# Memory attention and an erf-softplus feed-forward layer: the summed keys and values turned by VectorE's block transposes, phi's maxima spread through a row in device memory

## The chip, the core and the metric

The kernel runs on one core of a Trainium2 chip. The metric is the device time of one execution in microseconds; before the change it is 703.14 us, the median of 3 runs (702.33 to 703.39). One execution was also recorded by the hardware profiler; every time below that is not the median comes from that execution.

## What is computed

```python
def _attn_ref(q, k, v, phi):                 # batch 8, heads 8, seq 576, head_dim 64, 32 memories
    a = phi - np.max(phi, axis=2, keepdims=True)
    a = np.exp(a)
    a = a / (np.sum(a, axis=2, keepdims=True) + 1e-09)
    k_m = np.einsum('bhsm,bhsd->bhmd', a, k)
    v_m = np.einsum('bhsm,bhsd->bhmd', a, v)
    scores = scale * np.matmul(q, k_m.transpose(0, 1, 3, 2))     # scale = 1/8
    scores = scores - np.max(scores, axis=-1, keepdims=True)
    attn = np.exp(scores)
    attn = attn / (np.sum(attn, axis=-1, keepdims=True) + 1e-09)
    return np.matmul(attn, v_m)
def _moe_ref(x, w_in, w_out):                # 4608 tokens, 512 -> 2048 -> 512
    h = x @ w_in
    sp = np.maximum(h, 0.0) + np.log1p(np.exp(-np.abs(h)))
    return (h * erf(sp)) @ w_out
```

For each batch and head, 32 weights per position (softmax of phi over the sequence) condense keys and values to 32 "memories"; the queries attend to these; the result goes through a two-layer network.

## The kernel before

The 8 batches are worked on one after the other in 16 steps each (128 steps in all): step k makes 128 of the 2048 hidden columns for the 576 positions of a batch. For a step TensorE makes `psh` (first layer, `ffn1`, line 794), ScalarE or VectorE copies it to `h` (lines 811, 812), ScalarE takes softplus and erf in groups of four steps (lines 829, 834), VectorE multiplies and splits the product into a rounded part and a remainder, `g_hi` and `g_lo` (lines 860 to 863), and some steps later TensorE adds the product with `w_out` into `pso`, one accumulator for each 128 positions (`ffn2`, line 871). The last 64 positions of two batches share `psr`. At a batch's end ScalarE copies each `pso` to a tile `ot` (line 931), and SyncE stores it; `ot` lies in the two buffers of the pool `phiT`.

Keys, values and phi of batch b are prepared while earlier batches run through the steps:

- VectorE takes phi's maxima `pmx` (line 502), for 128 rows (four heads of 32 memories) in each of two halves `g`. ScalarE spreads each along a row of 128 (`bias`, line 507), TensorE transposes the two halves (line 527), so that in PSUM the maxima of a head and memory stand in a column of every partition, and VectorE adds them to the phi that has the positions in the partitions (line 533); ScalarE takes exp (line 536).
- TensorE sums keys and values with these weights (`psa<-kv,phi`, line 621). ScalarE divides by the sum and writes each of the sums twice side by side (`kvk`, line 647). TensorE transposes four 128x128 blocks of it (line 653), and ScalarE copies the result out of PSUM into `km` (times the scale 1/8) and `vm` (line 678), two buffers each, one for each parity of b.
- From `km` TensorE makes the scores (`psa<-q,km`, line 691), VectorE turns them (line 739) and makes the softmax; from `vm` and `w_in` TensorE makes `vw` (line 691 too), which is split for the first layer.

The order on every engine is made ahead by a planner (`Plan.order`): each operation has a cost and a rank, and of those that are ready the one with the lowest rank goes next; a table of numbers moves single operations in rank. Each engine then executes its instructions strictly in this order, and each DMA is issued from SyncE's queue in its order.

Of the kernel before, what the change touches and what calls it, by code (L numbers as in the profile page):

```python
# [32 lines left out]
ROW = 116  # L33
# [215 lines left out]
def tile_memory_attention_then_erf_softplus_ffn(  # L249
# [36 lines left out]
    LAG = 6  # L286
    FR1, FR2 = 4, 6
    IN_PSUM = 1
    TAIL = 3
# [3 lines left out]
        for n, b, kw in (  # L293
# [7 lines left out]
            ("g", 3, {}),  # L301
            ("raw", RAW, {}),
            ("ps", 4, {"space": PSUM}),
            ("po", 1, {"space": PSUM}),
# [3 lines left out]
    room = {"wo": NPR, "vw_hi": 2, "vw_lo": 2, "at": 8, "h": HB, "e": EB}  # L308
    room.update({"g_hi": 3, "g_lo": 3, "raw": RAW, "ps": 4, "sc": 2, "dk": 1, "bias": 1, "phiT": 2})
    room.update({f"pso{d}": 1 for d in range(NT)})  # L310
# [43 lines left out]
    rest = const.tile([P, NK, 2, P], F32R, name="rest")  # L354
    km = [const.tile([P, NP_, M], F32, name=f"km{i}") for i in range(2)]
    vm = [const.tile([P, NP_, M], F32, name=f"vm{i}") for i in range(2)]
    w_in_sb = [const.tile([P, NP_, 512], F32, name=f"w_in{p}") for p in range(4)]
# [140 lines left out]
    def phi_sums(rank, b):  # L498

        for g in range(NG):  # L500
            t, mx = ("phiT", b, g), tile_(f"pmx{g}", "pmx", b, g)
            op(DVE, on_dve(S), rank, [t], [mx], lambda t=t, mx=mx: nc.vector.reduce_max(  # L502
                out=get(mx), in_=get(t), axis=AX.X, negate=True))
        if b:
            bias = tile_("bias", "bias", b, shape=[P, NG, P], pool="att")
            for g in range(NG):
                op(ACT, 320, rank, [("pmx", b, g)], [(bias, g)], lambda g=g: nc.scalar.activation(
                    get(bias)[:, g], ident, AF.Identity, scale=0.0, bias=get(("pmx", b, g))))
# [10 lines left out]

    def phi_numbers(rank, b):  # L520

        a, bias = ("phi", b), ("bias", b)
# [16 lines left out]
    def memories(rank, rank_2, b, parts):  # L539
# [3 lines left out]
        if b:  # L543
            together(rank, phi_numbers(rank, b))
        else:
# [7 lines left out]
        for turn_n, part in enumerate(parts):  # L553
            first, second = sums_and_turn(rank_2 + turn_n * 0.01, b, part)
            together(rank_2 + turn_n * 0.01, first)
            together(rank_2 + turn_n * 0.01, second)

    bundles = []

    def together(rank, *pieces, kind="small"):  # L560
# [35 lines left out]
    def sums_and_turn(rank, b, part, rank_2=None, into=None):  # L596
# [32 lines left out]
        kvs = [("kv", b, x, g) for g, x in part]  # L629

        def first():
            if into is None:
                tile_("ps", *ps, shape=[P, 4, P], pool="ps")
            tile_("dk", *t, shape=[P, 4, 2, D], pool="att")
            yield
            yield n_g * NC * 110 * n_x, [a] + kvs, [ps] if into is None else [(k, "sums") for k in banks], [t], sums
            for n, g in enumerate(gs):
                rs = ("prs", b, g)

                def keep(f, n=n):  # L640
                    return lambda: f(
                        get(t)[:, n * n_x : (n + 1) * n_x],
                        sums_of(n).rearrange("p (x d) -> p x d", d=D).unsqueeze(2)
                        .to_broadcast([P, n_x, 2, D]))

                op(ACT, on_act(2 * n_x * D, True), rank, [ps if into is None else (banks[n], "sums"), rs], [(t, n)],
                   keep(lambda y, x, rs=rs: nc.scalar.activation(y, x, AF.Identity, scale=get(rs))),
# [33 lines left out]

        return first(), second()

# [40 lines left out]
    def attention(rank, rank_2, u, more=0):  # L724
# [13 lines left out]
        for g in range(NG):  # L738
# [7 lines left out]
        op(ACT, on_act(S), rank_2, [s], [s],  # L746
           lambda: nc.scalar.activation(get(s), get(s), AF.Exp), kind="exp")
        op(DVE, on_dve(S), rank_2, [s], [sm], lambda: nc.vector.reduce_sum(
# [245 lines left out]

    def alone(rank, x):
        together(rank, x, kind=None)

# [28 lines left out]
    for b in range(1, B):  # L1026
        o = NK * b
        if b == 1:
            PARTS += [
                (o + 1, [(phi_numbers, 2), (vw, 1, 4)]),  # L1030
                (o + 5, [(sums[2],), (vw, 1, 8)]),
                (o + 5, [(turn[2],)]),
                (o + 9, [(attention, 4), (vw, 1, 12)]),
# [13 lines left out]
    for n, fs in PARTS:  # L1047
        when(int(n), bundle, at(n), fs)
    for b in range(1, B, 2):
        for k in range(0, NK, 2):  # L1050
# [25 lines left out]
    for n, d in {  # L1076
# [10 lines left out]
    }.items():  # L1087
        plan.ops[n].rank += d
    for n, e in {
        324: ACT, 382: ACT, 476: ACT, 516: ACT,  # L1090
    }.items():
        plan.ops[n].ways = {e: plan.ops[n].ways[e]}
# [64 lines left out]
```

## Time and profile before

| | |
|---|---|
| median of 3 runs | 703.14 us (702.33 to 703.39) |
| the profiled execution | 702.5 us |
| its span | 700.7 us |
| TensorE busy (matmul) | 694.5 us, 99% of the span |
| ScalarE busy | 490.7 us, 70% |
| VectorE busy | 451.5 us, 64% |
| DMA | 66.71 MB, mean 95 GB/s |

The span goes from the first to the last instruction of the program; the execution's own time has 1.8 us more around it. "Busy" is the union of an engine's recorded instructions. Matmuls overlap each other in the records: one starts long before the one ahead of it has ended, so what a matmul costs is seen from the distance between starts, not from its recorded length.

### The profile page before, as it was taken

The page shows a single profiled execution, that of the slowest core. Times are in us where ns is not written, and L with a number is a line of the kernel's source. Part 1 is how long each engine was busy: PE and PEld are TensorE (multiplying, and loading weights), DVE is VectorE, ACT ScalarE, POOL GpSimd, SP SyncE. Part 2 cuts the span into 40 slices and gives each one's busy share as a digit, 9 for nine tenths or more (in the row PEclk, how much of TensorE's full clock was granted, in tenths as well). Part 3 has the DMA queues.
Part 4 walks back from the last instruction along what each step waited for, and adds up shares of the span by engine and source line. Part 5 has one row for each costly group of instructions (what it writes and reads, how often), then busy time and mean ns, then how long its engine had stood idle before and what let it go on. Part 6 is the DMA issues. An engine that isn't in the chain of part 4 may idle for free.

```text
span 700.7 us, 12333 instructions
## 1 busy us (share of the span) xinstructions
PE 694.5 (99%) x4866; PEld 562.8 (80%) x4866; DVE 451.5 (64%) x779; ACT 490.7 (70%) x797; POOL 105.9 (15%) x262
## 2 busy tenths in 40 slices
PE   8999999999999999999999999999999999999997
PEld 4566778788887888878888788878888788888886
DVE  4999999687744567685554747665565258546530
ACT  4899998967766678788655777586576557566821
POOL 0024111111101111121111110211111012111110
PEclk9999999999999999999999999999999999999999
DMA  9999131615103041113310323010010100000002
GB/s 362 415 417 415 53 125 52 236 36 198 59 1 102 7 189 46 54 64 108 116 35 0 110 98 136 24 61 1 2 50 19 61 16 1 1 37 24 1 1 75
DMA packets 19993, 66.71 MB, mean 95 GB/s; under 512 B 2272, under 2 KB 2528, under 8 KB 19936
## 3 DMA queue, kind: packets, MB, share of 16 engines
q1 hardware_dynamic: 19504, 64.85, 25.0%
q10 hardware_dynamic: 432, 1.08, 0.4%
q8 instruction: 38, 0.62, 0.3%
q14 instruction: 19, 0.16, 0.1%
HBM read 56.49 MB, written 9.44 MB: 94 GB/s over the span
## 4 chain that ended last, share of the span: by engine, by line
PE 92%; DVE 4%; DMA 2%; ACT 1%; issue 0%
PE pso L871 50%; PE psh L794 28%; PE psr L871 6%; PE psa L691 5%; PE psa L621 2%; DMA q<-qT 2%; DVE w L453 1%; DMA phiT<-phiT 1%; PE psa L653 0%; DVE w L477 0%; DVE g L849 0%; DVE h L811 0%; DVE w_in L477 0%; DVE phi L533 0%; DVE pmx L502 0%
## 5 line engine op out<-in xcount | busy, mean ns | idle before, releaser
L871 PE MATMUL pso<-wo,g_hi 128*128 128x512 f32 x976 | 305.9, 395 | 0.1
L871 PEld LDWEIGHTS pso<-wo,g_hi 128*128 128x128 f32 x976 | 174.8, 188 | 44.2 <-issue 12.6
L871 PE MATMUL pso<-wo,g_lo 128*128 128x512 f32 x488 | 191.6, 393 | 0.0
L812 ACT ACTIVATE h<-psh 128x288 f32<-128x288 f32 x176 | 71.5, 410 | 116.0 <-PE psh L794 115.2
L867 POOL CAST rest<-g_hi 128x64 fp32r<-128x64 f32 x122 | 51.5, 424 | 435.8 <-DVE g_hi L862 420.4
L860 DVE TENSOR_TENSOR e<-e,h 128x576 f32<-128x576 f32 x122 | 90.6, 754 | 34.0 <-ACT e L834 33.6
L794 PE MATMUL psh<-at_hi,vw_hi 128*128 128x288 f32 x496 | 108.7, 300 | 0.0
L871 PEld LDWEIGHTS pso<-wo,g_lo 128*128 128x128 f32 x488 | 91.6, 188 | 21.0
L794 PE MATMUL psh<-at_lo,vw_hi 128*128 128x288 f32 x496 | 106.3, 296 | 0.0
L794 PE MATMUL psh<-at_hi,vw_lo 128*128 128x288 f32 x496 | 105.8, 295 | 0.0
L862 DVE CAST g_hi<-e 128x576 fp32r<-128x576 f32 x122 | 54.8, 454 | 76.5 <-PE pso L871 67.5
L794 PEld LDWEIGHTS psh<-at_hi,vw_hi 128*128 128x128 f32 x496 | 86.1, 188 | 17.2 <-issue 3.0
L863 DVE TENSOR_TENSOR g_lo<-e,g_hi 128x576 fp32r<-128x576 f32 x122 | 93.6, 771 | 6.3
L829 ACT ACTIVATE e<-h 128x576 f32<-128x576 f32 x127 | 86.3, 685 | 14.4 <-DVE g_lo L863 8.3
L834 ACT ACTIVATE e<-e 128x576 f32<-128x576 f32 x128 | 81.1, 678 | 0.4
L794 PEld LDWEIGHTS psh<-at_hi,vw_lo 128*128 128x128 f32 x496 | 79.9, 189 | 0.0
L794 PEld LDWEIGHTS psh<-at_lo,vw_hi 128*128 128x128 f32 x496 | 79.2, 188 | 0.0
L811 DVE COPY h<-psh 128x288 f32<-128x288 f32 x78 | 34.3, 449 | 38.7 <-PE psh L794 38.5
L867 POOL CAST rest<-g_lo 128x64 fp32r<-128x64 f32 x122 | 44.4, 365 | 92.1 <-DVE g_lo L863 90.2
L369 DVE TENSOR_TENSOR vw_lo<-psa,vw_hi 128x512 fp32r<-128x512 f32 (+1 forms) x68 | 41.1, 638 | 15.1 <-ACT vw_hi L367 15.1
L871 PE MATMUL psr<-wo,rest 128*128 128x512 f32 x192 | 46.1, 390 | 0.0
L367 ACT ACTIVATE vw_hi<-psa 128x512 fp32r<-128x512 f32 (+1 forms) x68 | 34.3, 562 | 14.5 <-PE psa L691 14.5
(83 smaller groups left out, 646.3 us busy)
## 6 DMA issues: line engine op xcount, KB each, us to landing
kv<-kv SPq DMA_DIRECT2D x31, 640.0 KB, 8.5
w<-w_in SPq DMA_DIRECT2D x8, 1023.8 KB, 14.8
w<-w_out SPq DMA_DIRECT2D x8, 1023.8 KB, 14.6
q<-qT SPq DMA_DIRECT2D x28, 288.0 KB, 3.1
out<-ot SPq DMA_DIRECT2D x31, 256.0 KB, 2.2
phi<-phi SPq DMA_DIRECT2D x7, 640.0 KB, 4.5
phiT<-phiT SPq DMA_DIRECT2D x15, 288.0 KB, 3.0
q<-qT SPq DMA_DIRECT2D x2, 576.0 KB, 10.3
```

Source lines behind the costliest of these rows:

```text
L367: lambda: nc.scalar.activation(get_hi(), get_src(), AF.Identity))
L369: lambda: nc.vector.tensor_tensor(out=get_lo(), in0=get_src(), in1=get_hi().bitcast(F32), op=ALU.subtract))
L691: nc.tensor.matmul(out=get(ps[par])[p * M : (p + 1) * M, :n], lhsT=w[rows, p, :], rhs=x_of(rows, p), start=True, stop=True,)
L794: nc.tensor.matmul(out=get(ps)[:, :U], lhsT=x[:, g, k % 4 * P : (k % 4 + 1) * P], rhs=y[:, g, :], start=(n + g == 0), stop=(n == len(parts ...
L812: other={ACT: (on_act(U, True), lambda: nc.scalar.activation(keep(), get(ps), AF.Identity))})
L829: last[:] = [op(ACT, on_act(S), rank, [("h", i)], [e], lambda: nc.scalar.activation(get(e), get(("h", i)), AF.Softplus), kind="softplus", ...
L834: last[:] = [op(ACT, on_act(S), rank, [e], [e], lambda: nc.scalar.activation(get(e), get(e), AF.Erf), kind="erf", edge=edge, after=last)]
L860: op(DVE, on_dve(S), rank, [e, h], [e], lambda: nc.vector.tensor_tensor(out=get(e), in0=get(e), in1=get(h), op=ALU.mult))
L862: op(DVE, on_dve(S, 1), rank, [e], [hi], lambda: nc.vector.tensor_copy(out=get(hi), in_=get(e)))
L863: op(DVE, on_dve(S), rank, [e, hi], [lo], lambda: nc.vector.tensor_tensor(out=get(lo), in0=get(e), in1=get(hi).bitcast(F32), op=ALU.subtract))
L867: lambda x=x, y=y: nc.gpsimd.tensor_copy(out=rest[:, k, x, cols], in_=get(y)[:, NT * P :]))
L871: nc.tensor.matmul(out=o, lhsT=y, rhs=z, start=(start and n == 0), stop=(stop and n == len(parts) - 1))
```

## The change

For batches 2 to 7 (`TURNED = 2`) the four TensorE transposes of `kvk` and the four ScalarE copies out of PSUM are left out. ScalarE writes the sums once into `kvk`, not twice, and VectorE turns it by eight block transposes (32 partitions, 4 blocks of 32 each) straight into `kvm`, a tile that now holds km and vm side by side. The scale 1/8 moves into the exp of the scores. For batches 3 to 7 (`SPREAD = 3`) the maxima go through device memory: SyncE writes the two columns `pmx` into a `row` of 256 numbers, then loads it into all 128 partitions as `bias`; VectorE adds this from SBUF. ScalarE's two spreads and TensorE's two transposes for it are left out. The table of ranks and the list of engines are replaced.

```diff
+    TURNED, SPREAD = 2, 3
+            ("row", 2, {"space": bass.MemoryType.DRAM}),
-    km = [const.tile([P, NP_, M], F32, name=f"km{i}") for i in range(2)]
-    vm = [const.tile([P, NP_, M], F32, name=f"vm{i}") for i in range(2)]
+    kvm = [const.tile([P, 2, NP_, M], F32, name=f"kvm{i}") for i in range(2)]
+    km, vm = ([t[:, x] for t in kvm] for x in range(2))
...
-        if b:
+        if b >= SPREAD:
+            bias = tile_("bias", "bias", b, shape=[P, NG * P], pool="att")
+            row = tile_("row", "row", b, shape=[NG, P], pool="row")
+            for g in range(NG):
+                op(SP, 60, rank, [("pmx", b, g)], [(row, g)], lambda g=g: nc.sync.dma_start(
+                    out=get(row)[g].unsqueeze(1), in_=get(("pmx", b, g))), nbytes=P * 4)
+            op(SP, 60, rank, [row], [bias], lambda: nc.sync.dma_start(
+                out=get(bias), in_=get(row).rearrange("g p -> (g p)").unsqueeze(0)
+                .to_broadcast([P, NG * P])), nbytes=P * P * 8)
+        elif b:
...
+        if b < SPREAD:
+            return phi_numbers_turned(rank, b)
+        a, bias = ("phi", b), ("bias", b)
+        op(DVE, on_dve(NC * H * M), rank, [a, bias], [a], lambda: nc.vector.tensor_tensor(
+            out=get(a)[:ROW], in0=get(a)[:ROW],
+            in1=get(bias)[:ROW].unsqueeze(1).to_broadcast([ROW, NC, H * M]), op=ALU.add))
+        op(ACT, on_act(NC * H * M), rank, [a], [a], lambda: nc.scalar.activation(
+            get(a)[:ROW], get(a)[:ROW], AF.Exp), kind="exp")
...
+        def turned():
+
+            for j in range(4):
+                for d in range(2):
+                    to = slice((j % 2 * 2 + d) * 32, (j % 2 * 2 + d + 1) * 32)
+
+                    def emit(j=j, d=d, to=to):
+                        nc.vector.transpose(
+                            out=kvm[b % 2][to, :, j // 2 :: 2].rearrange("p x g m -> p g x m"),
+                            in_=get(t)[M * j : M * (j + 1), :, 0, d * 32 : (d + 1) * 32]
+                            .rearrange("p (g x) d -> p g x d", x=2))
+
+                    op(DVE, on_dve(4 * M), rank_2, [(t, n) for n in range(2)],
+                       [((name, b % 2), (j // 2, j % 2, d)) for name in ("km", "vm")], emit)
+
...
-        return first(), second()
+        return first(), turned if b >= TURNED else second()
...
-           lambda: nc.scalar.activation(get(s), get(s), AF.Exp), kind="exp")
+           lambda: nc.scalar.activation(get(s), get(s), AF.Exp, scale=SCALE if b >= TURNED else 1.0),
...
-        98: -50, 107: 1523, 109: -4304, 124: -81, 142: 741, 147: 235, 155: 1600, 157: 322,
...
+        90: 54, 98: -511, 104: -2, 109: -5919, 116: -385, 120: -617, 121: -744, 122: -1929,
...
-        324: ACT, 382: ACT, 476: ACT, 516: ACT,
+        45: DVE, 324: ACT, 452: ACT, 492: DVE, 516: ACT, 1418: DVE, 2298: DVE,
```

The order on TensorE where the sums of batch 2 are made, near 126 us. `psa<-kv,phi` are the sums, `psa<-w_in,vm` is a piece of `vw`, `psa<-ident,kvk` are the transposes. Before:

```order
L621 MATMUL psa<-kv,phi 32x128 x40
L691 MATMUL psa<-w_in_101,vm_98 32x512 x8
L653 MATMUL psa<-ident,kvk 128x128 x4
L871 MATMUL pso<-wo,g_hi 128x512 x2
L871 MATMUL pso<-wo,g_lo 128x512
L794 MATMUL psh<-at_hi,vw_hi 128x288 x2
```

And after:

```order
L654 MATMUL psa<-kv,phi 32x128 x40
L740 MATMUL psa<-w_in_101,kvm_98 32x512 x8
L844 MATMUL psh<-at_hi,vw_hi 128x288 x2
L844 MATMUL psh<-at_lo,vw_hi 128x288 x2
L844 MATMUL psh<-at_hi,vw_lo 128x288 x2
L921 MATMUL pso<-wo,g_hi 128x512 x2
```

The four transposes are gone, and first-layer matmuls now stand ahead of the second layer's.

The order on VectorE after the change, in the same stretch (before it, none of the block transposes is there, and the addition to phi of batch 3 is 10 rows further on, behind the turned scores `sc`):

```order
L671 STREAM_TRANSPOSE kvm_97<-kvk 32x2x2x32 x5
L371 TENSOR_TENSOR vw_lo<-psa,vw_hi 128x512 x2
L671 STREAM_TRANSPOSE kvm_97<-kvk 32x2x2x32 x3
L861 COPY h<-psh 128x288 x2
L526 TENSOR_SCALAR psm<-psm 128x1
L536 TENSOR_TENSOR phi<-phi,bias 116x1280
L528 RECIPROCAL prs<-psm 128x1
L910 TENSOR_TENSOR e<-e,h 128x576
L788 STREAM_TRANSPOSE sc<-psa 128x288 x2
```

Eight block transposes and the addition of batch 3 now stand ahead of the next product `e` and of the turned scores.

The order of SyncE's queue from 97 us on. Before:

```order
L429 DMA q<-qT 128x576 x4
L418 DMA kv<-kv 128x1280
L934 DMA out<-ot 128x512 x2
L412 DMA phi<-phi 128x1280
L418 DMA kv<-kv 128x1280 x4
```

And after:

```order
L431 DMA q<-qT 128x576 x4
L510 DMA row<-pmx 128x1
L420 DMA kv<-kv 128x1280
L510 DMA row<-pmx 128x1
L512 DMA bias<-row 128x256
L984 DMA out<-ot 128x512 x2
L414 DMA phi<-phi 128x1280
L420 DMA kv<-kv 128x1280 x4
```

The three transfers of batch 3's maxima stand around the last load of batch 2's keys and values and ahead of the first two stores of batch 0's result.

## Rows read from the trace of the kernel before

**Rows 1.** The page of the profiled execution: busy time of each engine with its share of the span and its instructions, and the chain of work that ended last, by engine.

```profile
PE 694.5 (99%) x4866; PEld 562.8 (80%) x4866; DVE 451.5 (64%) x779; ACT 490.7 (70%) x797; POOL 105.9 (15%) x262
...
PE 92%; DVE 4%; DMA 2%; ACT 1%; issue 0%
```

**Rows 2.** The waits of all engines: who waited for whom, us in total, how often, the longest. The first is the only wait of a matmul for anything but the very start.

```profile
PE psa L691 <- DMA q<-qT: 0.7, 1, 0.7
ACT h L812 <- PE psh L794: 115.2, 114, 4.0
DVE g_hi L862 <- PE pso L871: 67.5, 27, 4.9
```

**Rows 3.** Busy time by stretch (start:end in us, its length, then busy us and instructions of each engine, granted TensorE clock, DMA share, GB/s).

```profile
80.00:122.00 42.00, 42.00 (x259) 34.73 (x259) 41.89 (x69) 39.17 (x63) 6.83 (x16) 1.00 0.23 73
122.00:140.00 18.00, 17.88 (x203) 13.85 (x203) 11.70 (x26) 17.68 (x30) 3.07 (x7) 1.00 0.65 241
240.00:400.00 160.00, 160.00 (x1145) 133.78 (x1145) 101.59 (x186) 115.21 (x182) 23.05 (x61) 1.00 0.23 79
```

**Rows 4.** TensorE's timeline about the transposes of batch 7's `kvk`: start us, length us, line, operation, tiles, count.

```profile
500.36 0.62 PE L871 MATMUL pso<-wo,g_hi 128*128 128x512 f32 x2
500.82 0.39 PE L871 MATMUL pso<-wo,g_lo 128*128 128x512 f32 x1
...
503.33 0.60 PE L653 MATMUL psa<-ident,kvk 128*128 128x128 f32 x4
503.69 0.70 PE L871 MATMUL pso<-wo,g_hi 128*128 128x512 f32 x2
504.23 0.40 PE L871 MATMUL pso<-wo,g_lo 128*128 128x512 f32 x1
```

**Rows 5.** The same about the transposes of batch 4's `bias`.

```profile
226.45 0.38 PE L527 MATMUL psa<-ident,bias 128*128 128x128 f32 x2
226.58 0.51 PE L794 MATMUL psh<-at_hi,vw_hi 128*128 128x288 f32 x2
226.93 0.42 PE L794 MATMUL psh<-at_lo,vw_hi 128*128 128x288 f32 x2
227.19 0.43 PE L794 MATMUL psh<-at_hi,vw_lo 128*128 128x288 f32 x2
```

**Rows 6.** All engines' timeline about the transposes of batch 2's `kvk`; in brackets the idle time before an instruction, and what ended it.

```profile
129.26 0.66 PE L653 MATMUL psa<-ident,kvk 128*128 128x128 f32 x4
129.68 0.71 PE L871 MATMUL pso<-wo,g_hi 128*128 128x512 f32 x2
130.22 0.39 PE L871 MATMUL pso<-wo,g_lo 128*128 128x512 f32 x1
...
130.34 1.29 DVE L369 TENSOR_TENSOR vw_lo<-psa,vw_hi 128x512 fp32r<-128x512 f32 x2 [2.45 <-ACT vw_hi L367]
...
132.22 0.30 PEld L871 LDWEIGHTS pso<-wo,g_hi 128*128 128x128 f32 x2 [0.54 <-ACT ot L931]
```

**Rows 7.** Groups of instructions by line and shape: count, busy us in all, mean ns of one, then idle us before them.

```profile
L653 PE MATMUL psa<-ident,kvk 128*128 128x128 f32 x32 | 5.3, 279 | 0.1
L527 PE MATMUL psa<-ident,bias 128*128 128x128 f32 x14 | 2.7, 271 | 0.0
L739 DVE STREAM_TRANSPOSE sc<-psa 128x288 f32<-128x288 f32 x32 | 13.5, 460 | 15.2 <-PE psa L691 14.7 <-ACT kvk L647 0.4
L760 DVE STREAM_TRANSPOSE f<-sc 128x576 f32<-128x576 f32 x14 | 10.8, 774 | 0.1
L533 DVE TENSOR_TENSOR phi<-phi,psa 116x1280 f32<-116x1280 f32 x7 | 10.4, 1480 | 0.0
L369 DVE TENSOR_TENSOR wo<-w,wo 128x1024 fp32r<-128x1024 f32 x7 | 8.5, 1212 | 0.0
L507 ACT ACTIVATE bias<-ident,pmx 128x128 f32<-128x128 f32 x14 | 5.5, 404 | 1.7 <-DVE pmx L502 1.7
```

**Rows 8.** DMA issues: kind, queue, count, KB each, median us from issue to landing.

```profile
kv<-kv SPq DMA_DIRECT2D x31, 640.0 KB, 8.5
phi<-phi SPq DMA_DIRECT2D x7, 640.0 KB, 4.5
out<-ot SPq DMA_DIRECT2D x9, 128.0 KB, 2.3
```

**Rows 9.** All engines' timeline between 116 and 137 us, picked rows of SyncE's queue (SPq), ScalarE and VectorE.

```profile
116.55 0.33 SPq L418 DMA_DIRECT2D kv<-kv  x1
116.80 0.75 DVE L502 TENSOR_REDUCE pmx<-phiT 128x1 f32<-128x576 f32 x1
...
121.19 0.35 SPq L934 DMA_DIRECT2D out<-ot  x1
...
127.09 0.58 ACT L931 ACTIVATE ot<-pso 128x512 f32<-128x512 f32 x1
...
128.15 0.37 SPq L412 DMA_DIRECT2D phi<-phi  x1
...
134.72 0.46 DVE L811 COPY h<-psh 128x288 f32<-128x288 f32 x1 [2.72 <-PE psh L794]
```

**Rows 10.** Timelines of ScalarE and TensorE for batch 5: the last copies of its turned sums, and the first use of `km`.

```profile
337.71 0.26 ACT L678 ACTIVATE vm<-psa 64x128 f32<-64x128 f32 x1
...
355.77 0.71 PE L691 MATMUL psa<-q,km 64*32 64x288 f32 x16
```

More of the change, by code (lines that the diff above doesn't have):

```diff
@@ L308, in tile_memory_attention_then_erf_softplus_ffn @@
     room = {"wo": NPR, "vw_hi": 2, "vw_lo": 2, "at": 8, "h": HB, "e": EB}
-    room.update({"g_hi": 3, "g_lo": 3, "raw": RAW, "ps": 4, "sc": 2, "dk": 1, "bias": 1, "phiT": 2})
+    room.update({"g_hi": 3, "g_lo": 3, "raw": RAW, "ps": 4, "sc": 2, "dk": 1, "bias": 1, "phiT": 2, "row": 2})
     room.update({f"pso{d}": 1 for d in range(NT)})
@@ L520, in phi_numbers, with phi_numbers_turned @@
     def phi_numbers(rank, b):
+        if b < SPREAD:
[6 more added lines that the diff above has]
+            get(a)[:ROW], get(a)[:ROW], AF.Exp), kind="exp")
+    def phi_numbers_turned(rank, b):
         a, bias = ("phi", b), ("bias", b)
@@ L543, in memories @@
         if b:
-            together(rank, phi_numbers(rank, b))
+            alone(rank, phi_numbers(rank, b), "small")
         else:
@@ L555, in memories, with alone @@
             together(rank_2 + turn_n * 0.01, first)
-            together(rank_2 + turn_n * 0.01, second)
+            if b >= TURNED:
+                second()
+            else:
+                together(rank_2 + turn_n * 0.01, second)
     bundles = []
+    def alone(rank, x, kind=None):
+        if x is None:
+            return
+        if callable(x):
+            x()
+        else:
+            together(rank, x, kind=kind)
     def together(rank, *pieces, kind="small"):
@@ L633, in first @@
                 tile_("ps", *ps, shape=[P, 4, P], pool="ps")
-            tile_("dk", *t, shape=[P, 4, 2, D], pool="att")
+            y_n = 1 if b >= TURNED else 2
+            tile_("dk", *t, shape=[P, 4, y_n, D], pool="att")
             yield
@@ L643, in keep @@
                         sums_of(n).rearrange("p (x d) -> p x d", d=D).unsqueeze(2)
-                        .to_broadcast([P, n_x, 2, D]))
-                op(ACT, on_act(2 * n_x * D, True), rank, [ps if into is None else (banks[n], "sums"), rs], [(t, n)],
+                        .to_broadcast([P, n_x, y_n, D]))
+                op(ACT, on_act(y_n * n_x * D, True), rank, [ps if into is None else (banks[n], "sums"), rs], [(t, n)],
                    keep(lambda y, x, rs=rs: nc.scalar.activation(y, x, AF.Identity, scale=get(rs))),
@@ L746, in attention @@
         op(ACT, on_act(S), rank_2, [s], [s],
-           lambda: nc.scalar.activation(get(s), get(s), AF.Exp), kind="exp")
+           lambda: nc.scalar.activation(get(s), get(s), AF.Exp, scale=SCALE if b >= TURNED else 1.0),
+           kind="exp")
         op(DVE, on_dve(S), rank_2, [s], [sm], lambda: nc.vector.reduce_sum(
@@ L993, in bundle @@
             f(rank, *args) if f is phi_numbers else f for f, *args in fs))
-    def alone(rank, x):
-        together(rank, x, kind=None)
     sums, turn = {}, {}
@@ L1029, in tile_memory_attention_then_erf_softplus_ffn @@
             PARTS += [
-                (o + 1, [(phi_numbers, 2), (vw, 1, 4)]),
+                (o + 1, [(phi_numbers, 2)] * (SPREAD > 2) + [(vw, 1, 4)]),
                 (o + 5, [(sums[2],), (vw, 1, 8)]),
-                (o + 5, [(turn[2],)]),
+                *([] if TURNED <= 2 else [(o + 5, [(turn[2],)])]),
                 (o + 9, [(attention, 4), (vw, 1, 12)]),
@@ L1048, in tile_memory_attention_then_erf_softplus_ffn @@
         when(int(n), bundle, at(n), fs)
+    if TURNED <= 2:
+        when(NK + 5, alone, at(NK + 5), turn[2])
+    if SPREAD <= 2:
+        when(NK + 1, phi_numbers, at(NK + 1), 2)
     for b in range(1, B, 2):
```

21 rows, old and new, of the table g are left out of this document.

## The prediction, made before the changed kernel was run

> **What bounds the kernel.** First the page: TensorE's matmuls fill 694.5 of 700.7 us, and 92% of the chain that ended last is TensorE's [rows 1]. Then the waits: once the kernel has begun, a matmul waits for another engine's data 0.7 us in all, for a load of queries at the start. The others wait for TensorE: ScalarE 115.2 us for `psh`, VectorE 67.5 us for `pso` [rows 2]. Last the stretches: from 240 to 400 us TensorE is busy all the time, VectorE 101.59 and ScalarE 115.21 of 160 us; only from 80 to 122 us is VectorE as full, with 41.89 of 42 us [rows 3]. So TensorE's stream of instructions sets the end. A transpose that leaves it is worth what it adds to the distance between its neighbours' starts, as long as nobody makes TensorE wait instead. One wait is almost there already: at 132.22 us a weight load for `pso` waited for the copy of `pso` to `ot` [rows 6].
>
> **What is removed.** Batches 3 to 7 lose four transposes of `kvk` each. At 503.33 us these hold the next matmul up to 503.69, 0.36 us, and that pair of `pso` takes 0.54 us from its start to the third matmul (503.69 to 504.23), where an ordinary pair takes 0.46 (500.36 to 500.82) [rows 4]: 0.44 us a batch, 2.2 us for five. Batch 2's stand behind a piece of `vw`: 129.26 to 129.68, then the same long pair (to 130.22) [rows 6], 0.42 + 0.08 = 0.50 us. The two transposes of `bias` take 0.13 us (226.45 to 226.58), and the pair of `psh` behind them 0.35 us, where the next takes 0.26 [rows 5]: 0.22 us, for batches 3 to 7 1.1 us. Together 2.2 + 0.5 + 1.1 = 3.8 us. No other matmul is added or left out; the reordering changes a few neighbours, which I cost at nothing, because in the rows the pairs differ in length behind a transpose only.
>
> ScalarE loses ten spreads at 0.404 us [rows 7] and 24 copies at 0.26 us [rows 10], 10.3 us, gains one table load, and writes half as much into `kvk`. TensorE does not wait for it in general [rows 2], so I cost this at nothing. The exp with a scale is the same instruction.
>
> **What is added on VectorE.** 48 block transposes of 128 elements. The nearest rows have 288 elements in 0.460 us and 576 in 0.774 us [rows 7], a slope of 1.09 ns an element on 0.146 us: 0.29 us as an estimate, 2.3 us a batch, 14 us in all. The bounds: 0.14 us by the slope alone, 0.46 us as for 288. I take the middle, since the pattern is the same operation on fewer elements. The addition to phi reads SBUF, not PSUM: 1.480 us before; the nearest row with both inputs in SBUF, 1.212 us for 1024 elements [rows 7], gives 1.51 us for 1280, no difference.
>
> These are hidden where VectorE idles: 37% of the time from 240 to 400 us [rows 3]. The tight place is batch 2, where 2.3 us of transposes and 1.5 us of batch 3's addition come between 129 and 137 us. VectorE idled 2.45 us before 130.34 [rows 6] and 2.72 us before 134.72 [rows 9], so 3.8 us fit into 5.2; over 122 to 140 us it is busy 11.70 of 18 [rows 3]. By the upper bound it is 3.7 + 1.5 = 5.2 us, and the cover is just used up; then the copies of `h` and the product behind it are late next. For the other batches `km` is not needed at once: batch 5's last copy begins at 337.71 us, and `psa<-q,km` at 355.77 [rows 10], 18 us of room.
>
> A rule of the Trainium skill weighs on the first term. VectorE: DVE Perf Modes, The three transpose paths, gives 390 ns for a 128x128 transpose on TensorE and 311 ns on VectorE. By 390 ns the 34 transposes would be worth 13.3 us, by the starts in this trace they are worth 3.8; the trace does not agree, because there a transpose starts long before the one ahead of it has ended.
>
> **What is added on SyncE.** Per batch two writes of 512 B and a load of 128 KB that waits for both. The trace has no such write; the nearest rows are the stores of 128 KB, 2.3 us to landing, and above them the key and value loads, 8.5 us [rows 8]. I take 2.3 us for each of the two that follow one another, 4.6 us. Batch 3's second maximum ends at 116.80 + 0.75 = 117.55 us [rows 9], and its addition stands behind block transposes that can't begin before about 129.3 us, when `kvk` is there [rows 6]: 11.7 us or more of cover. For batches 4 to 7 the addition stands at least three steps behind the maxima, 3 x 5.5 us (700.7 / 128). Behind the waiting load in SyncE's queue are two stores, then phi of batch 3, issued at 128.15 us before [rows 9]; with 4.5 us to landing [rows 8] it is there at 132.7. Its addition comes behind the eight transposes (129.3 + 2.3 us), 1.29 us of `vw_lo` [rows 6] and two copies of `h`, that is at about 133.8 us: it waits for neither transfer, but only by 1.1 us.
>
> **The sum.** 702.5 - 3.8 = 698.7 us for an execution like the profiled one. The median of the runs is 703.14, 0.6 us above that execution, so I predict 703.14 - 3.8 = 699.3 us. The wait at 132.22 us (0.54 us of weight load) may go, since four copies leave ScalarE's queue ahead of it, or be paid again by a softmax exp of phi that stands there now; I leave it out.
>
> **The rivals.**
>
> *The load of `bias` holds up the stores.* The first store of `ot` goes out at 121.19 us, behind a 640 KB load issued at 116.55 [rows 9]. If the tiny writes queue behind that load, they land no sooner than 116.55 + 8.5 = 125.1 us; add 2.3 us, and the load of `bias` and the store behind it go at about 127.4 us. Store and `ot` share two buffers, so the next copy, at 127.09 us [rows 9], would wait for a landing at 129.7 us: ScalarE stands 2.6 us, with erf and the accumulators' release behind it. For it: the copy of `pso` is what TensorE waited for at 132.22 [rows 6]. Against it: it happens for batch 3 alone; later maxima have no such load ahead. It takes 1 to 2.6 us back: 700.3 to 701.9 us. The Trainium skill, DMA: Bandwidth & Descriptors, Specifications, says that transfers under 512 B read, modify and write; no run so far shows how much longer 128 writes of 4 B take.
>
> *VectorE's runs of transposes make TensorE wait (slower).* Eight in a row plus the addition, 3.8 us, release nothing that TensorE needs. If `h` copies and `g` products come late by that, TensorE loses its four PSUM tiles. It decides from 0.63 us lost in each of the six batches (3.8 / 6). At half a run, 1.9 us, it is 11.4 us, and the time 699.3 + 11.4 = 710.7 us. For it: a run at the upper bound uses up all cover of batch 2. Against it: VectorE itself waits for TensorE 67.5 us at `g_hi` [rows 2].
>
> *Nothing comes of it.* The pace is set by the softplus and erf chain, TensorE's free time turns into waits, 703 us. For it: VectorE full from 80 to 122 us [rows 3]. Against it: nothing but the order changes before 122 us, and after it ScalarE waits for `psh` rather than the reverse.
>
> *The transposes block TensorE for their whole recorded length*, 24 x 0.279 + 10 x 0.271 us [rows 7] = 9.4 us: 693.7 us. Against it: the starts, 0.36 us for four [rows 4]. By the Trainium skill's 390 ns (the page and section named above) it would be 13.3 us and 689.2 us.
>
> **How the numbers follow.** What a measurement here can tell from no change is about 0.2%, 1.4 us, so faster means under 701.7 us. The forecast holds with 0.67, between 698.2 and 700.3 us; the stores' rival 0.15, three quarters of it under 701.7; VectorE's 0.09, half of it slower by over 0.2%, half within; nothing comes of it 0.06; whole lengths 0.03. Faster: 0.67 + 0.11 + 0.03 = 0.81; within 0.14; slower 0.05. The range leaves out the last three, 0.18, and reaches from 698.2 (the forecast with 0.5 us of wait gone and 0.6 us of block that I priced too low) to 701.9 us, the end of the stores' rival.
>
> **What will show it.** Right: in the profile of the changed kernel TensorE's idle time stays as it was, its matmuls' busy time is down by about 3.8 us with the span, and the block transposes take 0.25 to 0.35 us. Wrong: waits of `pso` for `ot` or of `psh` for `h` near 125 to 140 us, or a `phi` addition on VectorE that waits for a DMA. A median above 701.7 us would say that the time freed on TensorE was given back as such waits.

## The result: slower by 1%, and the profile after

The changed kernel takes 710.32 us (median of 4 runs, 709.16 to 710.72), the kernel before 702.80 beside it: ratio 1.0104, 95% interval 1.0089 to 1.0119. Predicted were 699.3 us, 698.2 to 701.9. The profiled span grew from 700.7 to 708.9 us. The page after, beside [rows 1]: TensorE's busy time, its granted clock in 40 slices (17.7 us each), and the chain that ended last.

```profile
PE 694.2 (98%) x4832; PEld 562.7 (79%) x4832; DVE 464.5 (66%) x823; ACT 483.2 (68%) x768; POOL 107.9 (15%) x262
...
PEclk9999999889999999999999999999999999999999
...
PE 80%; DVE 11%; DMA 5%; issue 2%; ACT 2%; SPq 0%; DVEq 0%; ACTq 0%
```

TensorE has 34 matmuls fewer and is yet as busy as before. The clock's digit falls in two neighbouring slices, 124 to 159 us, and the chain has parts on VectorE and DMA that it had not. The waits after, of TensorE over the whole span (against 0.7 us in [rows 2]), of ScalarE and VectorE between 110 and 150 us, and of SyncE over the whole span:

```profile
PE psh L844 <- ACT vw_hi L369: 7.9, 1, 7.9
...
ACT ot L981 <- DMA out<-ot: 9.6, 1, 9.6
...
DVE kvm L671 <- ACT kvk L696: 10.5, 1, 10.5
...
SPq L512 <- DMA row<-pmx: 40.6, 5, 12.1
```

TensorE waits long at one place; its other waits behind the start are 0.8 us or less. The rows there, the after of [rows 9], from the timelines of SyncE's queue, ScalarE, VectorE and TensorE:

```profile
114.48 0.33 SPq L510 DMA_DIRECT2D row<-pmx  x1
116.36 0.33 SPq L420 DMA_DIRECT2D kv<-kv  x1
117.39 2.15 SPq L510 DMA_DIRECT2D row<-pmx  x1
131.79 0.33 SPq L512 DMA_DIRECT2D bias<-row  x1
132.22 0.38 SPq L984 DMA_DIRECT2D out<-ot  x1
...
136.99 0.60 ACT L981 ACTIVATE ot<-pso 128x512 f32<-128x512 f32 x1 [9.64 <-DMA out<-ot]
138.05 0.62 ACT L696 ACTIVATE kvk<-psa,prs 128x128 f32<-128x128 f32 x2
139.12 1.09 ACT L369 ACTIVATE vw_hi<-psa 128x512 fp32r<-128x512 f32 x2
...
138.70 1.56 DVE L671 STREAM_TRANSPOSE kvm<-kvk 32x128 f32<-32x128 f32 x5 [10.48 <-ACT kvk L696]
...
131.52 0.40 PE L921 MATMUL pso<-wo,g_lo 128*128 128x512 f32 x1
139.78 0.61 PE L844 MATMUL psh<-at_hi,vw_hi 128*128 128x288 f32 x1 [7.86 <-ACT vw_hi L369]
```

Read it in order. SyncE issues the first column of batch 3's maxima, the 640 KB load of `kv`, and the second column. The load of `bias` waits for both columns and goes out at 131.79 us. The store of `ot` behind it, issued at 121.19 before [rows 9], goes out at 132.22. ScalarE's next copy to `ot` needs that store's buffer and begins at 136.99 instead of 127.09. Behind it on ScalarE stand `kvk` and `vw_hi`, and TensorE stands from 131.9 to 139.8 us. The 640 KB load, issued 1.9 us behind the first column, lands after 10.6 us; before, it took 3.8. The chain from 110 to 150 us, by its longest pieces (start, length), says the same:

```profile
117.39 14.34 DMA row<-pmx
...
132.22 4.67 DMA out<-ot
```

What comes behind the wait costs too. By stretch, in the columns of [rows 3], first the kernel before, then the changed one:

```profile
115.00:125.00 10.00, 10.00 (x60) 9.07 (x59) 10.00 (x19) 9.91 (x15) 1.79 (x5) 1.00 0.26 93
131.00:140.00 9.00, 8.88 (x70) 6.31 (x69) 5.16 (x13) 8.90 (x16) 0.24 (x1) 1.00 0.94 379
140.00:147.00 7.00, 7.00 (x47) 6.49 (x46) 6.99 (x12) 2.97 (x6) 0.24 (x1) 1.00 0.28 89
```

```profile
115.00:125.00 10.00, 10.00 (x60) 9.08 (x59) 9.53 (x18) 9.88 (x15) 1.78 (x5) 1.00 0.61 29
131.00:140.00 9.00, 1.14 (x5) 0.63 (x4) 1.24 (x5) 3.01 (x7) 0.00 (x0) 0.78 0.30 91
140.00:147.00 7.00, 7.00 (x27) 5.48 (x29) 5.66 (x12) 6.86 (x11) 0.00 (x0) 0.55 1.00 396
```

From 140 to 147 us TensorE is busy throughout, at a granted clock of 0.55: most of the stretch at the lower of its two levels, 1.2 GHz, after eight idle microseconds. And from 115 to 125 us the DMA engines are busy 0.61 of the time, against 0.26, while they move 29 GB/s, against 93. The DMAs of the row, answering [rows 8] (count, KB each, median us from issue to landing):

```profile
bias<-row SPq DMA_DIRECT2D x5, 128.0 KB, 4.5
row<-pmx SPq DMA_DIRECT2D x10, 0.5 KB, 7.6
```

VectorE's new instructions, in the columns of [rows 7], cost what the prediction gave them:

```profile
L671 DVE STREAM_TRANSPOSE kvm<-kvk 32x128 f32<-32x128 f32 x48 | 14.4, 301 | 11.3 <-ACT kvk L696 10.5
L536 DVE TENSOR_TENSOR phi<-phi,bias 116x1280 f32<-116x1280 f32 x5 | 7.4, 1481 | 0.0
```

### The profile page after: what moved, and what is told of

It is laid out like the page before. It is cut to its first block, busy times and chain, and to the rows that moved or that the text cites. A ratio compares the mean times of both kernels' runs of the same rounds, so it can differ in the third digit from the quotient of the medians.

```text
span 708.9 us, 12322 instructions
## 1 busy us (share of the span) xinstructions
PE 694.2 (98%) x4832; PEld 562.7 (79%) x4832; DVE 464.5 (66%) x823; ACT 483.2 (68%) x768; POOL 107.9 (15%) x262
## 4 chain that ended last, share of the span: by engine, by line
PE 80%; DVE 11%; DMA 5%; issue 2%; ACT 2%; SPq 0%; DVEq 0%; ACTq 0%
PE pso L921 44%; PE psh L844 24%; PE psr L921 6%; PE psa L740 4%; DMA row<-pmx 2%; DMA q<-qT 2%; PE psa L654 2%; DVE w L455 2%; DVE g_lo L913 1%; DVE wo L371 1%; DVE e L910 1%; DVE w L479 1%; DVE g_hi L912 1%; DMA out<-ot 1%; DVE vw_lo L371 1%
## 5 line engine op out<-in xcount | busy, mean ns | idle before, releaser
L921 PEld LDWEIGHTS pso<-wo,g_hi 128*128 128x128 f32 x976 | 176.9, 189 | 44.6 <-issue 9.2
L862 ACT ACTIVATE h<-psh 128x288 f32<-128x288 f32 x180 | 73.4, 410 | 111.8 <-PE psh L844 111.7
L917 POOL CAST rest<-g_hi 128x64 fp32r<-128x64 f32 x122 | 50.0, 412 | 441.9 <-DVE g_hi L912 438.0
L917 POOL CAST rest<-g_lo 128x64 fp32r<-128x64 f32 x122 | 48.9, 404 | 91.8 <-DVE g_lo L913 82.9
L861 DVE COPY h<-psh 128x288 f32<-128x288 f32 x74 | 32.6, 446 | 35.5 <-PE psh L844 35.4
```

Source lines behind the costliest of these rows:

```text
L861: lambda: nc.vector.tensor_copy(out=keep(), in_=get(ps)),
L862: other={ACT: (on_act(U, True), lambda: nc.scalar.activation(keep(), get(ps), AF.Identity))})
L917: lambda x=x, y=y: nc.gpsimd.tensor_copy(out=rest[:, k, x, cols], in_=get(y)[:, NT * P :]))
L921: nc.tensor.matmul(out=o, lhsT=y, rhs=z, start=(start and n == 0), stop=(stop and n == len(parts) - 1))
```

## The experiments

Theory A: the store of `ot` stands behind the row's DMAs on SyncE, ScalarE behind the store, TensorE behind ScalarE, and the low clock behind that; the rest of the change is worth what was predicted. Theory B: VectorE's block transposes hold the work up. Theory C: the new order on TensorE is worse. All times stand beside runs of the kernel before on the same chip, median 702.33 to 702.55 us.

**Bias last.** Batch 3's load of `bias` behind the stores and loads that followed it; SyncE's queue, before the edit and with it:

```diff
-bias<-row; out<-ot x2; phi<-phi; kv<-kv x4
+out<-ot x2; phi<-phi; kv<-kv x4; bias<-row
```

> The changed kernel, with one instruction at another place: the load of bias of batch 3 stands on SyncE behind the two stores of out, the load of phi and the four loads of kv that stood behind it. Theory A (the store of out stood behind a load that waited 14.3 us for its row; ScalarE, then TensorE, stood behind the store, and the granted clock fell after that): the 8 us of idle TensorE at 131.5 us and the stretch at a clock of 0.55 behind it are gone, so 710.3 - 8 - 3 = 699.3 us (698 to 701). Theory B (VectorE's block transposes and additions hold the chain up): VectorE's work is the same, 710 us. Theory C (the order that the table of numbers gives TensorE's work is worse): the order on TensorE is the same, 710 us.

Measured 708.0 us, ratio 1.0078 (1.0063 to 1.0093): 2.3 us better than the changed kernel, not 11, and between the theories' numbers, 699.3 and 710. The store now goes out in time, and still ScalarE gets its buffer late (SyncE and ScalarE, timeline):

```profile
121.52 0.34 SPq L985 DMA_DIRECT2D out<-ot  x1
...
133.69 0.60 ACT L982 ACTIVATE ot<-pso 128x512 f32<-128x512 f32 x1 [6.47 <-DMA out<-ot]
```

The store needs 12.1 us to land, where 2.3 is usual [rows 8]. B and C gain nothing from that, since the stall is still where A puts it; but the wait of the load of `bias` is the smaller part of it.

**Before and trip.** The kernel before, with batch 3's two column writes and a load of the row added ahead of the first store and used by nobody.

```diff
+    def round_trip():
+        for g in range(NG):
+            nc.sync.dma_start(out=row[g].unsqueeze(1), in_=get(("pmx", 3, g)))
+        nc.sync.dma_start(out=spare, in_=row.rearrange("g p -> (g p)")[: NG * 46]
+                          .unsqueeze(0).to_broadcast([P, NG * 46]))
...
+        if x in stores and not made.keys() & set(stores):
+            round_trip()
```

> The kernel before, with three DMAs more on SyncE and nothing else: just ahead of the first store of out, the two columns of maxima of batch 3 are written to a row in device memory and 92 of the 256 numbers are read back to all partitions, into a tile that nobody reads (47 KB, since on-chip memory has no room for 128). Theory A: the store waits for the row as in the changed kernel, and the whole loss appears without any of the change's gain: 702.8 + 8 + 3 = 713.8 us (711 to 715). Theories B and C: nothing of VectorE or of the order on TensorE differs from before, 702.8 us (702 to 704).

Measured 708.06 us, 1.008 (1.0063 to 1.0096). The three DMAs alone make a kernel slower that has neither block transposes nor a new order, against B and C. But it is 5.7 us, not 11, and TensorE's wait is 2.1 us of it:

```profile
PE psa L654 <- ACT kvk L648: 2.1, 1, 2.1
```

Two differences from the changed kernel are taken up below: `kv` stands ahead of both columns here, and the unused tile moved others.

**Trip in spare room.** The same, the unused tile in a pool of its own behind all others.

```diff
+            ("spare", 1, {}),
-        spare = pools["att"].tile([P, NG * 46], F32, name="spare", tag="spare")
+        spare = pools["spare"].tile([P, NG * 46], F32, name="spare", tag="spare")
```

> The kernel before with the same three DMAs as in the run before_and_trip, but the tile that nobody reads lies in a pool of its own behind all others, so that every other tile keeps its address; there it stood among the others and moved those behind it by 368 bytes. In that run TensorE waited 2.1 us, at one place, and yet the time rose by 5.7 us: against the kernel before, the rest came by itself, spread over the whole later run, 0.36 us at a time. Theory L (the addresses make the rest): 702.3 + 2.8 = 705 us (704.5 to 705.8). Theory M (something that the three DMAs leave behind makes it): 708 us again.

Measured 705.81 us (704.13 to 706.5), 1.0042 (1.0027 to 1.0057): theory L, at the end of its range: 2.2 us less with the other tiles at their old places. TensorE's longest wait is 1.3 us here. The largest group of matmuls, in the first run and in this one, against 305.9 us in the kernel before:

```profile
L872 PE MATMUL pso<-wo,g_hi 128*128 128x512 f32 x976 | 308.4, 397 | 0.3 <-ACT ot L932 0.3
```

```profile
L873 PE MATMUL pso<-wo,g_hi 128*128 128x512 f32 x976 | 306.0, 395 | 0.3 <-ACT ot L933 0.3
```

TensorE's busy time is 696.6 us in the first and 694.1 in this one. Only the second layer's matmuls are longer; those of the first layer are not. Why they are slower at the moved addresses stays open.

**Blocks only.** The maxima of all batches through TensorE.

```diff
-    TURNED, SPREAD = 2, 3
+    TURNED, SPREAD = 2, 8
```

> The changed kernel without the row: phi's maxima of all batches go through TensorE as before, VectorE's block transposes turn the sums of batches 2 to 7. The table of numbers is the changed kernel's. Theory A: no load of bias, so no stall; 24 of the 34 transposes are gone, the six groups of four at 0.44 us (0.50 in batch 2): 702.8 - 2.7 = 700.1 us (699 to 701.5). Theory B: all of VectorE's block transposes are there, 708 us or more. Theory C: the order on TensorE is nearly the changed kernel's, 709 us or more.

Measured 700.93 us, 0.9978 (0.9968 to 0.9987), inside A's range, though the gain of 1.4 us is half of the 2.7 that A gave: TensorE's busy time is down by 2.2 us, and 1.0 us of that came back as idle time. All 48 block transposes are there, and the kernel is faster: B falls. The table of numbers is there too, which speaks against C; the run with 128-byte pieces below settles it, with the changed kernel's order unchanged.

**Row only.** The sums turned by TensorE as before.

```diff
-    TURNED, SPREAD = 2, 3
+    TURNED, SPREAD = 8, 3
```

> The changed kernel without the block transposes: TensorE turns the sums of all batches as before, the maxima of batches 3 to 7 go through the row. The table of numbers is the changed kernel's, without its entries on the operations that differ. Theory A: the stall is there, and only the 10 transposes of the maxima (1.1 us) are saved: 702.8 - 1.1 + 11 = 712.7 us (710 to 714). Theory B: without the block transposes nothing is lost, 702 us. Theory C: 710 us or more, with no stall at the store of out.

Measured 712.56 us, 1.0152 (1.0129 to 1.0174), as A has it. TensorE's long wait is there again, now for `kvk`, which stands behind the same copy on ScalarE:

```profile
PE psa L704 <- ACT kvk L698: 6.5, 1, 6.5
```

**Rows last.** All three DMAs of batch 3 behind the seven; SyncE's queue:

```diff
-row<-pmx; kv<-kv; row<-pmx; bias<-row; out<-ot x2; phi<-phi; kv<-kv x4
+kv<-kv; out<-ot x2; phi<-phi; kv<-kv x4; row<-pmx x2; bias<-row
```

> The changed kernel, in which all three DMAs of batch 3's maxima (two writes of a column, one load) stand on SyncE behind the two stores of out, the load of phi and four loads of kv. With the load of bias alone moved, the store was issued at 121.5 us, its packets ran by 126, and still it landed only at 133.6. Theory A1 (the writes of 4 bytes themselves hold up what is queued behind them on their queue for about 7 us each; the load's wait is the smaller part): nothing urgent is behind them now, 702.3 - 3.8 + 0.5 = 699.0 us (698 to 700.5). Theory A2 (what holds up the store at 121 us is something else, as the load of kv just ahead of it): the store lands late as before, 707 us.

Measured 711.22 us, 1.0122 (1.0107 to 1.0137): missed, by another wait. The store is in time (the copy to `ot` begins at 127.32 us), as A1 said. But the columns, issued at 130.93 and 131.66 us behind four loads of `kv`, have landed only at 144.0, and VectorE's queue still has batch 3's addition early (VectorE's timeline, and TensorE's longest wait):

```profile
148.42 1.49 DVE L537 TENSOR_TENSOR phi<-phi,bias 116x1280 f32<-116x1280 f32 x1 [14.14 <-DMA bias<-row]
...
PE psh L845 <- DVE sc L789: 9.6, 1, 9.6
```

VectorE stands 14.1 us, and TensorE 9.6 us for a tile that VectorE empties behind it. A DMA that is moved in its queue must be followed to the engine that takes its result in order.

**Rows by GpSimd.** As bias last, with batch 3's two writes issued by GpSimd.

```diff
-nc.sync.dma_start(out=get(row)[g].unsqueeze(1), in_=get(("pmx", b, g)))
+(nc.gpsimd if b == 3 else nc.sync).dma_start(out=get(row)[g].unsqueeze(1), in_=get(("pmx", b, g)))
```

> The changed kernel with the load of bias of batch 3 moved back as in the run bias_last, and the two writes of batch 3's columns issued on GpSimd's queue at the time when SyncE issued them. Theory Q (the store waits because it stands behind the writes in one queue): the store lands in 2 to 3 us, 699 to 700.5 us. Theory E (the writes occupy the DMA engines themselves, whatever their queue): the store lands 8 to 12 us after its issue, 706 to 708 us.

Measured 708.4 us, 1.0087 (1.0071 to 1.0104): theory E, 0.4 us above its range. GpSimd, SyncE and ScalarE, timeline:

```profile
117.57 0.55 POOL L511 DMA_DIRECT2D row<-pmx  x1 [0.67 <-DVE pmx L505]
...
121.55 0.35 SPq L985 DMA_DIRECT2D out<-ot  x1
...
133.35 0.60 ACT L982 ACTIVATE ot<-pso 128x512 f32<-128x512 f32 x1 [6.10 <-DMA out<-ot]
```

SyncE has no tiny write ahead of the store, and the store needs 11.8 us all the same. So another issuer does not take the writes out of its way. (The large load still stands between the columns here; no run has the store behind the columns without it.) That is what the Trainium skill says (DMA: Bandwidth & Descriptors, Issuing engines are not separate DMA queues): DMAs of all issuers run on the same 16 engines; this run agrees.

**Kv ahead of both.** One load moved past one column; SyncE's queue:

```diff
-row<-pmx; kv<-kv; row<-pmx; bias<-row; out<-ot x2
+kv<-kv; row<-pmx x2; bias<-row; out<-ot x2
```

> The changed kernel, with the 640 KB load of kv that SyncE issued between batch 3's two column writes moved ahead of both; nothing else moves. In the runs before_and_trip, where kv stands ahead, both columns had landed 7 us after the second was issued; in the changed kernel it was 14.3 us. Theory K (a large load issued while the first column's 4-byte writes are in the DMA engines is slowed, and makes the second column late): the row lands at about 124.5 us, the store is issued then and lands at 129, ScalarE stands about 2 us and TensorE 1.3 us with no loss of clock: 699.2 + 0.2 + 1.3 = 700.7 us (700 to 702.5). Theory S (each column costs its 7 us wherever kv stands): the row lands at 131 us again, 709 to 711 us.

Measured 701.66 us, 0.9992 (0.9982 to 1.0002): theory K, 8.7 us better than the changed kernel by the place of one load. SyncE, ScalarE and TensorE:

```profile
116.28 0.33 SPq L420 DMA_DIRECT2D kv<-kv  x1
116.65 1.18 SPq L511 DMA_DIRECT2D row<-pmx  x2
124.76 0.32 SPq L513 DMA_DIRECT2D bias<-row  x1
125.19 0.37 SPq L985 DMA_DIRECT2D out<-ot  x1
...
129.85 0.60 ACT L982 ACTIVATE ot<-pso 128x512 f32<-128x512 f32 x1 [2.58 <-DMA out<-ot]
...
132.65 0.89 PE L845 MATMUL psh<-at_hi,vw_hi 128*128 128x288 f32 x2 [0.80 <-ACT vw_hi L369]
```

Both columns have landed 8.1 us after the first was issued (116.65 to 124.76), not 17.3 (114.48 to 131.79), and ScalarE stands 2.58 us, where the rival of the prediction had 2.6. This is the stall without the slowed load: `kv` lands after 4.0 us here. In the six runs in which it is issued about 2 us behind the first column it takes 9.8 to 10.6 us, in the runs in which it goes ahead of the row's writes 3.8 to 4.1. TensorE waits 0.8 us at this place and 0.2 us behind it; that explains less than half of the 2.3 us by which the next run is faster, and the rest stays open.

**Row in 128-byte pieces.** VectorE turns each column first, so that it leaves from 4 partitions.

```diff
+                    y = wide_of[b, g] = pools["wide"].tile([P, 32], F32, name="wide", tag=f"wide{g}")
+                    nc.vector.transpose(out=y, in_=get(mx).to_broadcast([P, 32]))
...
-                    out=get(row)[g].unsqueeze(1), in_=get(("pmx", b, g))), nbytes=P * 4)
+                    out=get(row)[g].rearrange("(n c) -> n c", c=32), in_=wide_of[b, g][::32]), nbytes=P * 4)
```

> The changed kernel, in which VectorE first turns each column of maxima (one 32x32 block transpose of the column repeated 32 times, for batches 3 to 7), so that a column is written to device memory from 4 partitions, 128 bytes of each, and not from 128 partitions, 4 bytes of each. Order of the queues as in the changed kernel. Theory D (the number of 4-byte pieces is what takes the 7 us): the writes land in 2 to 3 us, batch 3's store is not late, 699 us (698.3 to 700.5). Theory F (any small write that is read back from device memory takes as long): 706 to 711 us.

Measured 699.37 us (699.25 to 699.45), 0.9953 (0.9938 to 0.9968): theory D. Order and queues are those of the changed kernel, the bytes are the same:

```profile
117.85 0.54 SPq L517 DMA_DIRECT2D row<-wide  x1
120.77 0.33 SPq L519 DMA_DIRECT2D bias<-row  x1
121.74 0.34 SPq L991 DMA_DIRECT2D out<-ot  x1
...
127.35 0.58 ACT L988 ACTIVATE ot<-pso 128x512 f32<-128x512 f32 x1
```

The load goes out 2.9 us after the second column, before ScalarE has the store's data, and nobody waits. The ten more transposes take VectorE 0.212 us each. What cost the 7 us of a column was its form, 128 pieces of 4 bytes from 128 partitions. The edit makes the pieces fewer and larger at once, so it does not say how much each does. But number alone is not it: the stores of 256 KB are 128 rows of 2 KB and land after 2.2 us. B falls here as well, and C: every block transpose and the whole order of the changed kernel are in this run.

**Batch 3 by TensorE.** Only batches 4 to 7 through the row.

```diff
-    TURNED, SPREAD = 2, 3
+    TURNED, SPREAD = 2, 4
```

> The changed kernel with batch 3's maxima through TensorE as before, those of batches 4 to 7 through the row. Theory A: the one place where a store of out is queued behind the row's DMAs within the time that ScalarE has is gone: 702.3 - 3.8 + 0.2 = 698.7 us (698 to 700). A rival, that the later rows cost something too, if only at the clock or at the DMA queues: 700.9 (the run with the blocks only) or more.

Measured 699.20 us (699.06 to 699.39), 0.9951 (0.9936 to 0.9966). The whole loss is batch 3's. The later rows take up to 7.4 us to land as well, and nobody waits for them. This run and the one above are faster than both kernels, and 0.2 us apart, which can't be told from no difference.

**Tensor kept busy.** Matmuls of the identity ahead of the matmul that waited.

```diff
+            if (i, half) == (NK + 8, 0):
+                for _ in range(34):
+                    nc.tensor.matmul(out=get(ps)[:, :P], lhsT=ident, rhs=ident, start=True, stop=True)
```

> The changed kernel, with 34 matmuls of the identity with itself (128 columns each) put ahead of the matmul that stood 7.9 us behind ScalarE; they write to the tile that this matmul overwrites, and give the result nothing. Theory G (the idle stretch makes the clock fall, and the half clock behind it costs about 3 us by the changed kernel's rows, up to 4.2 by the run bias_last): with TensorE busy through the wait the granted clock stays near 1.00 and the time falls to 706.5 us (705.5 to 707.8). Rival (the low clock has another cause, or the matmuls end after the wait does and give it back): 709.5 us or more.

Measured 715.31 us, 1.018 (1.0163 to 1.0196). It tells nothing on the clock's price: the tile they write to was the one that ScalarE had yet to empty, so they waited 6.56 us themselves and came on top:

```profile
138.53 10.67 PE L843 MATMUL psh<-ident 128*128 128x128 f32 x68 [6.56 <-ACT kvk L696]
```

**Tensor busy through wait.** The same 34 in the bank of a tile that is already full.

```diff
+            if (i, half) == (NK + 7, 1):
+                for _ in range(34):
+                    nc.tensor.matmul(out=get(ps)[:, U : U + P], lhsT=ident, rhs=ident, start=True, stop=True)
```

> The changed kernel, with 34 matmuls of the identity with itself put behind the matmuls of the last psh tile ahead of the wait, into columns of that tile's bank which nobody reads; no wait stands ahead of them, where those of the run tensor_kept_busy waited themselves for ScalarE. At the full clock they last about 7.3 us of the 7.9 in which TensorE stood; the two pairs of pso matmuls behind them come later by as much. Theory G (the idle stretch makes the clock fall, which costs 3 to 4.2 us by the rows of the changed kernel and of the run bias_last): the granted clock stays near 1.00 from 131 to 150 us, and the time falls to 706.7 us (705.5 to 707.8), though TensorE does nothing more of use. Rival (the loss is all wait): 710 us, or more by what the matmuls overshoot.

Measured 708.03 us, 1.0078 (1.0061 to 1.0095): 2.3 us better than the changed kernel, the span 2.7 us (708.9 to 706.2); theory G gave 3 to 4.2, and the time is 0.2 us above its range. The same stretches as above:

```profile
131.00:140.00 9.00, 9.00 (x76) 8.73 (x75) 1.80 (x6) 3.57 (x9) 0.00 (x0) 1.00 0.51 118
140.00:147.00 7.00, 6.71 (x57) 4.40 (x57) 6.49 (x14) 6.94 (x11) 0.00 (x0) 1.00 1.01 408
```

The matmuls of no use took 7.75 us of the wait, the clock stayed at 1.00, and 57 matmul records lie where 27 lay. The DMA engines are as full from 140 to 147 us as in the changed kernel (1.01 against 1.00), so it is not their traffic that made the matmuls slow there. The same instructions, from the first `psh` behind the wait to the first scores, in the changed kernel and in this run:

```profile
139.78 1.09 PE L844 MATMUL psh<-at_hi,vw_hi 128*128 128x288 f32 x2 [7.86 <-ACT vw_hi L369]
...
146.96 0.72 PE L740 MATMUL psa<-q,kvm 64*32 64x288 f32 x16
```

```profile
139.68 0.42 PE L844 MATMUL psh<-at_hi,vw_hi 128*128 128x288 f32 x2
...
144.24 0.71 PE L740 MATMUL psa<-q,kvm 64*32 64x288 f32 x16
```

They take 7.18 us and 4.56 us: 2.6 us. That part of the loss was the clock.

## Why the prediction was wrong

**What failed is one term: the writes on SyncE.** "The trace has no such write; the nearest rows are the stores of 128 KB, 2.3 us to landing": by size a safe bound, by pieces none. Those stores consist of rows of 1 or 2 KB, a column of 128 pieces of 4 bytes. A column took 7.6 us to land in the median; with the 640 KB load between the two of batch 3 the second one took 14.3. The load of `bias`, the other half of the term, took 4.5 us, not 2.3, and the store issued 0.4 us behind it 4.67; where no load of `bias` stood ahead of that store and the columns were out of the way, it took 2.1 us (rows last). The text named the row that it is nearest to in kind (a write) and left out that no row showed 4-byte pieces, so the upper end of this term was not bounded at all. The price alone would have kept the time in the stated range: with columns at 7.1 and 7.8 us but the load ahead of them, the run's median is 701.66 us, and the range ends at 701.9. What took it out is that the load between the columns made the second one late, and the low clock behind the stall; the sum had neither. The Trainium skill would not have helped by its figure: a fixed cost of about 2.0 us and the bytes behind it, for a DMA that GpSimd issues (DMA: Bandwidth & Descriptors, Anatomy of one DMA), gives 2.0 us as an estimate for 512 bytes. The columns that GpSimd issued took 8.7 and 15.1 us, and the measured times decide. Nor is its mark of 512 bytes, which the prediction cites, the whole of it: pieces of 128 bytes lie under it as well.

**The rival with the right mechanism was priced at a quarter.** "The load of `bias` holds up the stores" names the batch, the queue, the copy of `pso` and ScalarE. Its sum took the row's landing at 127.4 us and the store's at 2.3 us; measured were 131.7 and 4.67, so ScalarE stood 9.6 us and not 2.6. The run with `kv` ahead of both gives the 2.6 us of the sum, but by luck: the row was there at 124.8 us, not 127.4, and the store took 4.56 us, not 2.3. The sum let the tiny writes wait for the load, and took for it the median of all such loads, 8.5 us; this one had landed after 3.8 us in the kernel before. The runs show the reverse: the load itself is held up among the tiny writes, with the DMA engines busy 0.61 of the time from 115 to 125 us and 29 GB/s moved. And nothing in it asked what eight idle microseconds do to TensorE's clock: 2.3 to 2.7 us more.

**A number that came out by luck.** The rival of VectorE's runs of transposes gave 710.7 us, and 710.32 were measured. Its mechanism fell all the same: the blocks alone are faster than the kernel before. One figure of another rival is slightly off: 13.3 us less is 689.8 us on the base of 703.14, not 689.2.

**The account.** From the version with 128-byte pieces, 699.37 us, to the changed kernel's 710.32 are 10.9 us: 7.9 of wait, 2.3 to 2.7 by the clock, and a rest of 0.3 to 0.7 that no row explains.

**TensorE's transposes: right, a fifth too high.** 3.8 us were predicted. With the stall out of the way, the version with 128-byte pieces is 3.0 us under the kernel before beside it (702.39), its span 3.1 us shorter. TensorE's busy time is down by 3.5 us, from 694.5 to 691.0; the 0.4 us between the two came back as idle time. The forecast of 699.3 us is the time of the two versions without the stall, partly by luck: it was reached from a median of 703.14, above the 702.4 of the later runs, so that a base and a gain that were both too high cancel.

**VectorE: right.** 0.301 us a block transpose against 0.29, 1.481 us the addition against 1.51; in the blocks alone no wait of TensorE for VectorE is over 0.3 us. The cover in batch 2, which was feared to be too small, held: with 128-byte pieces VectorE is busy 7.49 us from 132 to 140 us, and TensorE all 8. **The condition set for being wrong** (waits between 125 and 140 us that lead back to `ot`) is what the trace shows.

## What to carry to other kernels

Price a transfer by the number and size of its pieces in memory, not by its bytes alone; if no row shows pieces of that size, the term's upper end is open, and the question is who stands behind it in the queue and on the DMA engines. A few hundred bytes from many partitions are better gathered into some rows on the chip first: 0.2 us on VectorE took 5 to 11 us off the landing. A stall of the engine that sets the end is to be priced with the clock that it has afterwards.

## What the runs showed of the hardware

A column of 128 pieces of 4 bytes took 7.6 us in the median to land in device memory; one of 4 pieces of 128 bytes was followed by the load that waits for it after 1.6 to 2.9 us. A 640 KB load issued between two such columns landed after 9.8 to 10.6 us instead of 3.8 to 4.1 and made the second column land after 14.3; a store issued 4 us behind the three landed after 12, even when another engine had issued the columns. In the changed kernel the DMA engines showed 0.61 busy at 29 GB/s meanwhile. Eight idle microseconds of TensorE were followed by about seven at a granted clock of 0.55. And 368 bytes more in each partition in the middle of on-chip memory made the second layer's matmuls slower: 2.2 us in 700, cause open.
